# Sketch matrices loaded first, fewer zero matmuls, q in 256 B runs, single tasks for the q normalisation and new planner numbers, in a planned attention and channel-mix kernel

## The chip, the cores and the metric

The kernel runs on one core of one Trainium2 chip. The metric is device time in microseconds (us) of one execution. The span that a profile shows is about 1.8 us shorter than the time of the same execution (111.1 us of span against 112.87 us of time, for the kernel before). Engines are called PE (matmuls), PEld (PE's weight loads), DVE (vector), ACT (scalar), POOL (GpSimd) and SP (sync, which issues DMAs).

Executions of one kernel do not all take the same time here. The kernel before has runs of 112.4 to 113.8 us, fast, and others of 114.3 to 115.6 us, slow. The first measurements of before, from which the prediction started, were all of 114.2 us or more. The mean granted clock of a profile is given where it is below 0.99.

## The reference, cut to what matters

```python
# q, k, v: (4 batches, 4 heads, 1088 tokens, 32), float32; S1, S2: (8, 32)
def phi(x):                                   # 64 features a token
    a, b = x @ S1.T, x @ S2.T
    return outer(a, b).reshape(..., 64)
q_p, k_p = phi(q), phi(k)
kv, z = k_p.T @ v, sum(k_p, tokens)           # per batch and head
attn = (q_p @ kv) / (q_p @ z + 1e-6)
x = attn, heads side by side                  # (4, 1088, 128)
xk = mu_k * x + (1 - mu_k) * x_prev           # x_prev: the token before
xr = mu_r * x + (1 - mu_r) * x_prev
out = sigmoid(xr @ w_r) * (relu(xk @ w_k)**2 @ w_v)      # 128 -> 1024 -> 128
```

## The kernel before

All work is cut into tasks. A small planner in the Python program (a list scheduler) takes for each task an engine, a cost in us, the tasks it depends on and sometimes a due date, and fixes the order of instructions on every engine. In the traces an instruction that waits holds back what stands after it on its engine: in before, ACT waits 1.46 us for zm ahead of a small copy (kvs, 65.24 us), and PP behind that copy starts at 65.35, though its matmuls had ended at 64.9. The name of a task tells its stage: KT (transpose of k), KP (projection of k), KF (features), KA (accumulate kv), KZ and KW (fold), QT (transpose of q), Q1 (projection of q), QN (normalise), QF (features), QX (attention output), XK (mix with the token before), M1 and RE and SQ and M2 (the two large matmuls with relu and square between), FN (output). In profile lines the tiles have names of their own: kT and qT are the transposed k and q, ps_kab and ps_abw their projections, kp and qp their features, ps_kv the sums for kv, ps_qtp the transposed qp, ps_x the attention output, ps_r the product for the sigmoid, zm the masked sums for kv, pw the first product of the normalisation, PP and XB the two results of ACT from the attention output (XK, the mixed rows, is made from ps_x and PP), ps_h the result of the first large matmul, k its relu and square, ps_o that of the second large matmul, osb the output product, wt the target of the zero matmuls, sps and sp the first products of the sketch matrices S1 and S2.

```python
class Plan:
    LAT = {"PE": 0.16, "ACT": 0.20, "DVE": 0.14, "DMA": 0.0}
    ...
        for t in reversed(order):            # a due date is handed back to what it needs
            d = 1e9 if t["due"] is None else t["due"]
            for s in succ[t["name"]]:
                d = min(d, s["d"] - s["us"] - self.LAT[s["eng"]])
            t["d"] = d
    ...
                    r = max(r, t["d"] - window - t["us"])          # not before its window
                    key = (max(r, clock[e] + 0.02), t["d"], t["i"]) # then the earliest due

def load_q(b, eng):                          # 34 tokens of 32 floats in a row: 4352 B runs
    eng.dma_start(hdq[b][:], q[b].rearrange("h (a t) d -> (h a) t d", a=32))

load_k(0, nc.sync)
nc.scalar.dma_start(S8[:, 0, :], S1); nc.scalar.dma_start(S8[:, 1, :], S2)
load_v(0, nc.sync); load_q(0, nc.sync)
...
def q_trans(b, hf):                          # two a batch; output stride is 34 floats
    o = qT[:, b * S:(b + 1) * S].rearrange("p (a t) -> p t a", t=2 * U)
    nc.vector.transpose(o[:, U * hf:U * hf + U], hdq[b][:, U * hf:U * hf + U, :])

def q_norm(g):                               # one task: four dependent operations in a row
    nc.vector.tensor_mul(pw[:, :n, :, :R], x[:, :, :, 1], wsb[g][:, :n])
    nc.vector.tensor_reduce(den[:, :n], pw[:, :n], axis=AX, op=ADD)
    nc.vector.reciprocal(den[:, :n], den[:, :n])
    nc.vector.tensor_mul(an[:, :n], x[:, :, :, 1], _ap(d_, ...))

T0, PER = 14.0, 1.95
...     add(f"FN{g}", "DVE", dve(N), ..., due=T0 + PER * (G0[g] + n) + 4)
seq = plan.run(7.0)                          # the window
pe = 1.6
for t in seq:
    if t["eng"] == "PE":
        if t["start"] < WARM:                # zero matmuls fill PE's planned gaps
            for _ in range(max(0, int((t["start"] - pe - 0.1) / 0.23))):
                nc.tensor.matmul(wt[:], zero[:, :P], zero[:], skip_group_check=True)
        pe = t["start"] + t["us"]
    if t["fn"]:
        t["fn"]()
```

The zero matmuls write a PSUM bank that nobody reads. They are there to keep PE active, so that its matmuls run at their faster spacing when real work comes; in before's trace the zero matmuls themselves start 0.43 us apart at first and 0.22 after the ninth.

Of the kernel before, what the change touches and what calls it, by code (L numbers as in the profile page):

```python
# [27 lines left out]
class Plan:  # L28

    LAT = {"PE": 0.16, "ACT": 0.20, "DVE": 0.14, "DMA": 0.0}  # L30

# [15 lines left out]
    def run(self, window):  # L47
# [31 lines left out]
        n = 0  # L79
        while n < len(order):  # L80
            best = None
            for e, ts in todo.items():
                cand = None
                for t in ts:
                    r = max(clock[e], t.get("rel", 0.0))
                    for d in t["deps"]:
                        if d not in done:
                            r = None
                            break
                        r = max(r, done[d])  # L90
                    if r is None:
                        continue
                    if t["opens"]:
                        fb = free[t["opens"][0]]
                        if not fb:
                            continue
                        r = max(r, min(fb.values()))
                    r = max(r, t["d"] - window - t["us"])
                    key = (max(r, clock[e] + 0.02), t["d"], t["i"])
                    if cand is None or key < cand[0]:  # L100
                        cand = (key, t, r)
                if cand and (best is None or cand[2] < best[2]):
                    best = cand
# [36 lines left out]
def kernel(  # L140
# [39 lines left out]
    warm = const.tile([R, 1], F32)  # L180
    zero = const.tile([P, 512], BF16)
    nc.vector.memset(warm[:], 0.0)
    nc.vector.memset(zero[:], 0.0)
    nc.scalar.activation(warm[:], warm[:], SIGMOID)

    hdk = [const.tile([P, 2, U, D], F32, name=f"hdk{b}") for b in range(B)]
    hdq = [const.tile([P, 2 * U, D], F32, name=f"hdq{b}") for b in range(B)]
    vt = [const.tile([P, H, 9, D], F32, name=f"vt{b}") for b in range(B)]
# [5 lines left out]

    def load_q(b, eng):
        eng.dma_start(hdq[b][:], q[b].rearrange("h (a t) d -> (h a) t d", a=32))

    def load_v(b, eng):
        src = v[b].rearrange("h (p u) d -> p h u d", u=U)
        eng.dma_start(vt[b][:64], src[:, :, :9])  # L200
        eng.dma_start(vt[b][64:, :, :8], src[:, :, 9:])

    load_k(0, nc.sync)
    nc.scalar.dma_start(S8[:, 0, :], S1)
    nc.scalar.dma_start(S8[:, 1, :], S2)
    load_v(0, nc.sync)
    load_q(0, nc.sync)
    for b in range(1, B):
        load_k(b, nc.sync)
        load_v(b, nc.sync)  # L210
        load_q(b, nc.sync)

# [80 lines left out]
    SZ = H * S * D * 4 / BW  # L293
    t_ = 3.5
    arr = {}
    for b in range(B):
        for x in "kvq":
            t_ += SZ
            arr[x + str(b)] = t_
            if (b, x) == (0, "q"):  # L300
                t_ += 3.6
                arr["w"] = t_
# [7 lines left out]
    for x in range(2):  # L310
        nc.vector.tensor_copy(sel2[:, x, x], id8)
    hm = lambda ap: ap.rearrange("p (h d) -> p h d", h=H)
    sp = psum.tile([P, 512], F32, name="sps", tag="a0")
# [47 lines left out]
    def k_feat(b, gi, t0, t1):  # L361
        ab = kab[b, gi]
        if t0 == 0:
            kkp[b, gi] = work.tile([P, 5, H, R, R], F32, name="kp", tag="kp", bufs=3)
# [52 lines left out]
    for b in range(B):  # L417
        prev = []
        for gi, (t0, t1) in enumerate(KG):
            n = t1 - t0  # L420
            x = f"{b}_{gi}"
            add("KT" + x, "DVE", 0.13 + 0.00104 * (n * 128) + 0.1, lambda b=b, gi=gi: k_trans(b, gi), [f"Lk{b}"])
            add("KP" + x, "PE", 0.13 * n + 0.1, lambda b=b, gi=gi: k_proj(b, gi), ["KT" + x], opens=("aux", "kab_" + x))
            add("KE" + x, "ACT", act(64 * n), lambda b=b, gi=gi: k_evac(b, gi), uses=["kab_" + x])
            parts = [(0, 2), (2, n)] if n == 4 else [(0, 3), (3, n)]
            for j, (p0, p1) in enumerate(parts):
                add(f"KF{x}_{j}", "DVE", dve(256 * (p1 - p0)), lambda b=b, gi=gi, p0=p0, p1=p1: k_feat(b, gi, p0, p1), ["KE" + x])
                nm = f"KA{x}_{j}"
                add(nm, "PE", 0.17 * (p1 - p0) + 0.2, lambda b=b, gi=gi, p0=p0, p1=p1: k_acc(b, gi, p0, p1),
                    [f"KF{x}_{j}", f"Lv{b}"] + prev, **(dict(uses=[f"kv_{b}"]) if prev else dict(opens=("kv", f"kv_{b}"))))  # L430
# [8 lines left out]
    def q_trans(b, hf):  # L439
        o = qT[:, b * S:(b + 1) * S].rearrange("p (a t) -> p t a", t=2 * U)  # L440
        nc.vector.transpose(o[:, U * hf:U * hf + U], hdq[b][:, U * hf:U * hf + U, :])  # L441

    for b in range(B):
        for hf in range(2):
            add(f"QT{b}_{hf}", "DVE", 0.08 + 0.00104 * 32 * U, lambda b=b, hf=hf: q_trans(b, hf), [f"Lq{b}"])

# [14 lines left out]
    def q_evac(g):  # L461
        n = GS[g]
        wsb[g] = work.tile([P, 4, H, R], F32, name="wsb", tag="wsb", bufs=3)
        nc.scalar.copy(wsb[g][:, :n], abw(g)[:, :, :, 2])

    def q_norm(g):
        n = GS[g]
        x = abw(g)
        pw = pws[g % 2]
        nc.vector.tensor_mul(pw[:, :n, :, :R], x[:, :, :, 1], wsb[g][:, :n])  # L470
        den = work.tile([P, 4, H], F32, name="den", tag="den")
        nc.vector.tensor_reduce(den[:, :n], pw[:, :n], axis=AX, op=ADD)
        nc.vector.reciprocal(den[:, :n], den[:, :n])
        d_ = den[:, :n]
        an = work.tile([P, 4, H, R], F32, name="an", tag="an")
# [3 lines left out]
    def q_feat(g, t0, t1):  # L479
        if t0 == 0:  # L480
            qp[g] = work.tile([P, 4, H, R, R], F32, name="qp", tag="qp", bufs=3)
# [97 lines left out]

    T0, PER = 14.0, 1.95  # L580
    for g in range(NG):
# [3 lines left out]
        ns = len(bs)  # L585
        add(f"Q1{g}", "PE", 0.17 * n + 0.15, lambda g=g: q_proj(g), [f"QT{b}_{hf}" for b in bs for hf in range(2)] + [f"KW{b}" for b in bs],
            opens=("aux", f"abw_{g}"))
        add(f"QE{g}", "ACT", act(32 * n), lambda g=g: q_evac(g), uses=[f"abw_{g}"])
        add(f"QN{g}", "DVE", 2 * dve(32 * n) + dve(36 * n) + dve(32 * n) + 0.05, lambda g=g: q_norm(g), [f"QE{g}"], uses=[f"abw_{g}"])
        parts = [(0, 1), (1, 2)] if n == 2 else [(0, 2), (2, 4)]  # L590
        for j, (p0, p1) in enumerate(parts):
            add(f"QF{g}_{j}", "DVE", dve(256 * (p1 - p0)), lambda g=g, p0=p0, p1=p1: q_feat(g, p0, p1), [f"QN{g}"], uses=[f"abw_{g}"])
        for pair in range(2):
# [4 lines left out]
                [f"QR{g}_{pair}"], uses=[f"qtp_{g}_{pair}"])  # L598
        add(f"QX{g}", "PE", 0.215 * n + 0.15, lambda g=g: q_x(g), [f"QV{g}_0", f"QV{g}_1"] + [f"KB{b}" for b in bs], opens=("aux", f"x_{g}"))
        add(f"XP{g}", "ACT", act(N, True) + 0.05 * (ns - 1), lambda g=g: x_pp(g), ["Lw"], uses=[f"x_{g}"])  # L600
        add(f"XK{g}", "DVE", dve(N) + 0.06 * (ns - 1), lambda g=g: x_xk(g), [f"XP{g}"], uses=[f"x_{g}"])
        add(f"XB{g}", "ACT", act(N) + 0.05 * (ns - 1), lambda g=g: x_xb(g), uses=[f"x_{g}"])
        for c in range(8):
            add(f"M1{g}_{c}", "PE", N / 2400 + 0.01, lambda g=g, c=c: mm1(g, c), [f"XK{g}"], opens=("h", f"h_{g}_{c}"))
            add(f"RE{g}_{c}", "ACT", act(N), lambda g=g, c=c: relu(g, c), uses=[f"h_{g}_{c}"])
# [8 lines left out]
    for n_, x_ in plan_arr.items():  # L614
        plan.ids["L" + n_]["rel"] = x_
    seq = plan.run(7.0)


    wt = psum.tile([P, 512], F32, name="wt", tag="o0")
    WARM = 17.0  # L620
    pe = 1.6
    for t in seq:
        if t["eng"] == "PE":
            if t["start"] < WARM:
                for _ in range(max(0, int((t["start"] - pe - 0.1) / 0.23))):
                    nc.tensor.matmul(wt[:], zero[:, :P], zero[:], skip_group_check=True)  # L626
            pe = t["start"] + t["us"]
# [32 lines left out]
```

## Time and profile before

| | before |
|---|---|
| time, median (first three runs) | 114.81 us |
| profiled span | 111.1 us |
| first k projection starts on PE | 12.12 us |
| first q product starts on DVE (pw) | 20.23 us |
| after that to the end | 90.87 us, of which DVE is busy 74.69, PE 77.25, ACT 64.12 |

The page of the profile. Part 1 gives busy us, share of the span and instructions of each engine; part 2 gives for 40 equal slices the busy tenths (9 is 90% or more), PEclk being the granted clock of PE:

```profile
span 111.1 us, 3029 instructions
PE 91.5 (82%) x1243; PEld 59.8 (54%) x1243; DVE 84.7 (76%) x192; ACT 67.2 (61%) x166; POOL 9.1 (8%) x27
...
PE   0689976996999997899999975999768499898960
...
DVE  6280296699999999899999994678996347967860
ACT  5000200345869733899696357999536799898950
...
PEclk9999999999999999999999999999999999999999
DMA  3999999998001003000030030000302000300311
```

One slice is 2.8 us. DVE has idle slices at the start, is full from the 9th to the 24th slice, and has holes after that; in the last third no engine is full throughout. The loads keep the DMA engines busy for ten slices, to about 28 us.

The timeline of the first 21 us (start us, us from the first start to the last end, engine, line, operation, operands, count, and in brackets the idle time before and who ended it):

```profile
6.29 5.90 PE L626 MATMUL wt<-zero 128*128 128x512 bf16 x19
7.12 1.48 DVE L343 STREAM_TRANSPOSE kT<-hdk 128x256 f32<-128x256 f32 x4
...
12.12 1.27 PE L350 MATMUL ps_kab<-SW,kT 128*64 128x64 f32 x36
...
13.26 2.85 DVE L333 TENSOR_TENSOR kp<-ab 128x512 f32<-128x512 f32 x4 [4.65 <-ACT ab L357]
...
16.04 2.21 DVE L441 STREAM_TRANSPOSE qT<-hdq 128x544 f32<-128x544 f32 x2
18.09 0.18 DVE L392 TENSOR_TENSOR zm<-ps_kv,mask 128x32 f32<-128x32 f32 x1
...
20.23 0.23 DVE L470 TENSOR_TENSOR pw<-ps_abw,wsb 128x64 f32<-128x64 f32 x1 [0.90 <-ACT wsb L464]
```

PE is in 19 zero matmuls until 12.1 us while the transposed k lies ready from 8.6 us. DVE waits 4.65 us for that. Later zm stands behind both q transposes, though it needs only the kv matmuls.

The chain of waits, a stretch of the last third (start us, us, what):

```profile
63.91 1.06 DVE qp L333 x2
...
65.03 0.18 DVE zm L392
65.21 2.14 DVE qT L441 x2
67.34 0.65 DVE XK L517 x2
...
68.03 0.39 PE ps_h L530
```

And of the view of waits, PE's longest one after the start (who <- whom: us in total, times, longest):

```profile
PE ps_h L530 <- DVE XK L517: 4.3, 4, 2.0
```

Here two q transposes of the next batch (2.14 us) stand in DVE's order before XK, which the large matmuls wait for. XK starts when the second one ends, and PE stands idle for 2.0 us ahead of ps_h. XK also waits for ACT. The timeline of ACT and DVE there and at the next such wait, which has no transpose ahead of XK:

```profile
65.35 0.84 ACT L512 ACTIVATE PP<-ps_x,omu_k 128x384 f32<-128x384 f32 x2
67.18 0.81 DVE L517 SCALAR_TENSOR_TENSOR XK<-ps_x,mu_k,PP 128x384 bf16<-128x384 f32 x2
...
85.27 0.84 ACT L512 ACTIVATE PP<-ps_x,omu_k 128x448 f32<-128x448 f32 x2 [0.44 <-PE ps_x L506]
86.68 0.88 DVE L517 SCALAR_TENSOR_TENSOR XK<-ps_x,mu_k,PP 128x448 bf16<-128x448 f32 x2 [1.50 <-ACT XB L523]
```

With DVE idle and ready, XK started 1.41 us after the start of its PP; behind the two transposes, 1.83 us after. So an estimate of the transposes' share in the 2.0 us is 0.4 us; the wait at 87.6 us, without them, was 1.6 us long.

Groups (busy us, mean ns of one | idle before them):

```profile
L542 DVE TENSOR_TENSOR k<-k 128x1024 bf16<-128x1024 bf16 (+1 forms) x40 | 23.6, 604 | 7.3 <-ACT k L536 6.6
L441 DVE STREAM_TRANSPOSE qT<-hdq 128x544 f32<-128x544 f32 x8 | 9.0, 1189 | 0.0
```

### The profile page before, as it was taken

What the parts mean: (1) busy time and instruction counts of PE and PEld (TensorE: products, weight loads), DVE (VectorE), ACT (ScalarE), POOL (GpSimd) and SP (SyncE); (2) the same over time, 40 slices, a digit from 0 to 9 for tenths busy, and PEclk for the clock granted to TensorE, in tenths of its full rate; (3) what the DMA queues carried; (4) which work ended last, traced back from release to release, by engine and by line L of the source; (5) the groups of instructions that cost most, each with busy time, mean ns of one, the idle gap of its engine ahead of it and who ended that gap; (6) DMA issues with size and microseconds to landing.
All of it is one profiled execution on the core that took longest, in us unless ns stands there. A gap on an engine that the chain in (4) does not pass through costs nothing.

```text
span 111.1 us, 3029 instructions
## 1 busy us (share of the span) xinstructions
PE 91.5 (82%) x1243; PEld 59.8 (54%) x1243; DVE 84.7 (76%) x192; ACT 67.2 (61%) x166; POOL 9.1 (8%) x27
## 2 busy tenths in 40 slices
PE   0689976996999997899999975999768499898960
PEld 0434562555466784638777753467645247366530
DVE  6280296699999999899999994678996347967860
ACT  5000200345869733899696357999536799898950
POOL 7390290000000000000000000000000000000000
PEclk9999999999999999999999999999999999999999
DMA  3999999998001003000030030000302000300311
GB/s 100 268 293 290 252 344 254 332 269 205 26 6 47 0 6 94 0 9 0 0 100 0 6 94 0 0 0 6 94 5 89 0 0 6 97 0 1 93 56 47
DMA packets 9166, 9.70 MB, mean 87 GB/s; under 512 B 1584, under 2 KB 7984, under 8 KB 9152
## 3 DMA queue, kind: packets, MB, share of 16 engines
q1 hardware_dynamic: 7840, 8.91, 28.1%
q0 software_dynamic: 1280, 0.59, 3.8%
q8 instruction: 10, 0.16, 0.7%
q14 instruction: 4, 0.03, 0.1%
q10 hardware_dynamic: 32, 0.00, 0.0%
HBM read 7.80 MB, written 2.23 MB: 90 GB/s over the span
## 4 chain that ended last, share of the span: by engine, by line
DVE 43%; PE 28%; ACT 18%; issue 5%; DMA 2%; DVEq 0%; ACTq 0%
ACT k L536 11%; DVE k L542 7%; DVE kp L333 7%; DVE qT L441 6%; PE wt L626 6%; DVE qp L333 5%; PE ps_h L530 4%; PE ps_x L506 4%; PE ps_o L552 3%; DVE osb L577 3%; DVE XK L517 3%; ACT PP L512 3%; DVE kT L343 3%; PE ps_kab L350 3%; DMA S<-in_S_dram 2%
## 5 line engine op out<-in xcount | busy, mean ns | idle before, releaser
L536 ACT ACTIVATE k<-ps_h 128x512 bf16<-128x512 f32 (+1 forms) x80 | 36.7, 558 | 3.4 <-PE ps_h L530 3.2
L542 DVE TENSOR_TENSOR k<-k 128x1024 bf16<-128x1024 bf16 (+1 forms) x40 | 23.6, 604 | 7.3 <-ACT k L536 6.6
L530 PE MATMUL ps_h<-XK,wk 128*128 128x512 bf16 (+1 forms) x80 | 21.9, 348 | 4.6 <-DVE XK L517 4.3
L552 PE MATMUL ps_o<-wv,k 128*128 128x128 bf16 x272 | 21.6, 220 | 1.6 <-DVE k L542 1.4
L552 PEld LDWEIGHTS <-k 128*128 128x128 bf16 x272 | 16.4, 98 | 7.6 <-DVE k L542 4.7
L333 DVE TENSOR_TENSOR kp<-ab 128x512 f32<-128x512 f32 (+1 forms) x16 | 11.7, 756 | 4.7 <-ACT ab L357 4.7
L530 PEld LDWEIGHTS <-wk 128*128 128x128 bf16 x80 | 6.6, 98 | 11.4 <-issue 9.4
L357 ACT COPY ab<-ps_kab 128x256 f32<-128x256 f32 (+1 forms) x8 | 3.3, 406 | 15.7 <-PE ps_kab L350 15.7
L489 PE MATMUL ps_qtp<-ident,qp 128*128 128x128 f32 x68 | 10.9, 283 | 1.9 <-DVE qp L333 1.2
L498 ACT COPY qpT<-ps_qtp 128x512 f32<-128x512 f32 (+1 forms) x18 | 9.2, 549 | 5.1 <-PE ps_qtp L489 5.1
L333 DVE TENSOR_TENSOR qp<-an,ps_abw 128x512 f32<-128x512 f32 (+1 forms) x20 | 11.2, 599 | 0.1
L489 PEld LDWEIGHTS ps_qtp<-ident,qp 128*128 128x128 f32 x68 | 7.3, 140 | 4.4 <-DVE qp L333 1.3
L517 DVE SCALAR_TENSOR_TENSOR XK<-ps_x,mu_k,PP 128x512 bf16<-128x512 f32 (+7 forms) x13 | 6.9, 552 | 3.5 <-ACT XB L523 2.2
L506 PE MATMUL ps_x<-qpT,kvbd 128*64 128x512 f32 (+7 forms) x52 | 9.5, 462 | 0.0
L378 PE MATMUL ps_kv<-kp,vt 128*32 128x64 f32 x288 | 7.2, 224 | 2.5 <-DVE kp L333 2.3
L441 DVE STREAM_TRANSPOSE qT<-hdq 128x544 f32<-128x544 f32 x8 | 9.0, 1189 | 0.0
L626 PE MATMUL wt<-zero 128*128 128x512 bf16 x28 | 8.5, 450 | 0.0
L512 ACT ACTIVATE PP<-ps_x,omu_k 128x512 f32<-128x512 f32 (+7 forms) x13 | 6.8, 548 | 2.5 <-PE ps_x L506 2.5
L454 PE MATMUL ps_abw<-SW,qT 128*64 128x96 f32 x136 | 7.6, 253 | 0.0
L378 PEld LDWEIGHTS ps_kv<-kp,vt 128*32 128x32 f32 x288 | 4.8, 109 | 5.1 <-DVE kp L333 4.1
L454 PEld LDWEIGHTS ps_abw<-SW,qT 128*64 128x64 f32 x136 | 5.9, 136 | 2.0 <-issue 0.6
L577 DVE TENSOR_TENSOR osb<-ps_o,r 128x512 f32<-128x512 f32 (+1 forms) x10 | 6.0, 604 | 0.8 <-PE ps_o L552 0.8
(69 smaller groups left out, 100.7 us busy)
## 6 DMA issues: line engine op xcount, KB each, us to landing
hdk<-in_k_dram SPq DMA_DIRECT2D x4, 544.0 KB, 9.7
hdq<-in_q_dram SPq DMA_DIRECT2D x4, 544.0 KB, 10.8
out_dram<-osb SPq DMA_DIRECT2D x7, 256.0 KB, 2.3
vt<-in_v_dram SPq DMA_DIRECT2D x4, 288.0 KB, 9.7
vt<-in_v_dram SPq DMA_DIRECT2D x4, 256.0 KB, 12.3
out_dram<-osb SPq DMA_DIRECT2D x3, 128.0 KB, 2.5
wk<-in_moe_w_k_dram POOLq DMA_DIRECT2D x1, 256.0 KB, 7.2
wv<-in_moe_w_v_dram POOLq DMA_DIRECT2D x1, 256.0 KB, 15.4
```

Of the source, the lines that this page charges most:

```text
L333: nc.vector.tensor_mul(o.rearrange("p t h i j -> p (t h) i j"), _ap(a_, [[sa, y], [1, R], [0, R]]), _ap(b_, [[sb, y], [0, R], [1, R]]))
L378: nc.tensor.matmul(kv[32 * h:32 * h + 32, :64], vt[b][:, h, T, :], kp[:, t, h].rearrange("p i j -> p (i j)"), start=(T == 0), stop=(T == 8 ...
L441: nc.vector.transpose(o[:, U * hf:U * hf + U], hdq[b][:, U * hf:U * hf + U, :])
L454: nc.tensor.matmul(p[64 * c:64 * c + 64, t * 96:t * 96 + 96], qT[:, s:s + 64], SW[:, s // S].rearrange("p h x r -> p (h x r)"), skip_group ...
L489: nc.tensor.transpose(p[:, t * P:t * P + P], qp[g][:, t, 2 * pair:2 * pair + 2].rearrange("p h i j -> p (h i j)"), ident[:])
L506: nc.tensor.matmul(p[64 * pair:64 * pair + 64, c0:c0 + m], kvbd[:, b, pair, :], qpT[g][:, pair, c0:c0 + m], skip_group_check=True, tile_po ...
L517: nc.vector.scalar_tensor_tensor(XK[:, s:s + m], tiles[f"x_{g}"][:, c0:c0 + m], mu_k[:], PP[:, c:c + m], op0=MUL, op1=ADD)
L530: nc.tensor.matmul(h[:, :n * P], wk[:, c * P:(c + 1) * P], XK[:, G0[g] * P:(G0[g] + n) * P])
L536: nc.scalar.activation(k1s[g, c // 2][:, c % 2, :n * P], tiles[f"h_{g}_{c}"][:, :n * P], RELU)
L542: nc.vector.tensor_mul(k2[:, :, :n * P], k1[:, :, :n * P], k1[:, :, :n * P])
L552: nc.tensor.matmul(o[:, t * P:t * P + P], k2s[g, j][:, c, t * P:t * P + P], wv[:, 2 * j + c, :], start=(j == 0 and c == 0 and t == 0), sto ...
L626: nc.tensor.matmul(wt[:], zero[:, :P], zero[:], skip_group_check=True)
```

## The change

Its intent: begin the serial start earlier, make the q transposes cheaper and smaller, let other work in between the small operations of the normalisation, and give the planner numbers meant to be nearer to the chip's.

```diff
-    LAT = {"PE": 0.16, "ACT": 0.20, "DVE": 0.14, "DMA": 0.0}
+    LAT = {"PE": 0.24, "ACT": 0.18, "DVE": 0.15, "POOL": 0.15, "DMA": 0.0}
+    OWN = {"PE": 0.0, "ACT": 0.15, "DVE": 0.12, "POOL": 0.12, "DMA": 0.0}
...
-                        r = max(r, done[d])
+                        r = max(r, done[d] - (self.LAT[e] - self.OWN[e] if self.ids[d]["eng"] == e else 0.0))
...
-        eng.dma_start(hdq[b][:], q[b].rearrange("h (a t) d -> (h a) t d", a=32))
+        for h in range(H):
+            engs[h % len(engs)].dma_start(hdq[b][32 * h:32 * h + 32].rearrange("a t c d -> a t (c d)"),
+                                          q[b, h].rearrange("(t a c) d -> a t (c d)", a=32, c=2))
...
+    nc.sync.dma_start(S8[:, 0, :], S1)
+    nc.scalar.dma_start(S8[:, 1, :], S2)
     load_k(0, nc.sync)
-    nc.scalar.dma_start(S8[:, 0, :], S1)
-    nc.scalar.dma_start(S8[:, 1, :], S2)
...
+    dummy(4)                     # four zero matmuls ahead of the sketch products
...
-        o = qT[:, b * S:(b + 1) * S].rearrange("p (a t) -> p t a", t=2 * U)
-        nc.vector.transpose(o[:, U * hf:U * hf + U], hdq[b][:, U * hf:U * hf + U, :])
+        o = qT[:, b * S:(b + 1) * S].rearrange("p (t a c) -> p t c a", a=32, c=2)
+        t0, t1 = QSP[hf]
+        nc.vector.transpose(o[:, t0:t1], hdq[b][:, t0:t1])
+    QSP = [(0, 4), (4, 9), (9, 13), (13, 17)]
...
-        add(f"QN{g}", "DVE", ..., lambda g=g: q_norm(g), ...)
+        add(f"QP{g}", ...); add(f"QD{g}", ...); add(f"QI{g}", ...); add(f"QN{g}", ...)
...
-    T0, PER = 14.0, 1.95
+    T0, PER = 8.0, 1.5
...                              # several task costs, for instance KP 0.13n -> 0.102n
-    seq = plan.run(7.0)
+    seq = plan.run(5.0)
...
-    WARM = 17.0
-    pe = 1.6
+    WARM = 14.0
+    pe = 4.4                     # 5 zero matmuls ahead of the first projection, where 19 were
```

A q projection now also waits only for the transposes whose tokens it needs.

More of the change, by code (lines that the diff above doesn't have):

```diff
@@ L181 @@
     zero = const.tile([P, 512], BF16)
+    nc.vector.memset(zero[:], 0.0)
     nc.vector.memset(warm[:], 0.0)
-    nc.vector.memset(zero[:], 0.0)
     nc.scalar.activation(warm[:], warm[:], SIGMOID)
     hdk = [const.tile([P, 2, U, D], F32, name=f"hdk{b}") for b in range(B)]
-    hdq = [const.tile([P, 2 * U, D], F32, name=f"hdq{b}") for b in range(B)]
+    hdq = [const.tile([P, U, 2, D], F32, name=f"hdq{b}") for b in range(B)]
     vt = [const.tile([P, H, 9, D], F32, name=f"vt{b}") for b in range(B)]
@@ L193, in load_k, with load_q @@
         eng.dma_start(hdk[b][:], k[b].rearrange("h (a c u) d -> (h a) c u d", a=32, c=2))
-    def load_q(b, eng):
-        eng.dma_start(hdq[b][:], q[b].rearrange("h (a t) d -> (h a) t d", a=32))
+    def load_q(b, engs):
+        for h in range(H):
+            engs[h % len(engs)].dma_start(hdq[b][32 * h:32 * h + 32].rearrange("a t c d -> a t (c d)"),
+                                          q[b, h].rearrange("(t a c) d -> a t (c d)", a=32, c=2))
     def load_v(b, eng):
@@ L201, in load_v @@
         eng.dma_start(vt[b][64:, :, :8], src[:, :, 9:])
+    nc.sync.dma_start(S8[:, 0, :], S1)
+    nc.scalar.dma_start(S8[:, 1, :], S2)
     load_k(0, nc.sync)
-    nc.scalar.dma_start(S8[:, 0, :], S1)
-    nc.scalar.dma_start(S8[:, 1, :], S2)
     load_v(0, nc.sync)
-    load_q(0, nc.sync)
+    load_q(0, [nc.sync, nc.scalar])
     for b in range(1, B):
@@ L210 @@
         load_v(b, nc.sync)
-        load_q(b, nc.sync)
+        load_q(b, [nc.sync])
     ident = const.tile([P, P], F32)
@@ L293 @@
     SZ = H * S * D * 4 / BW
-    t_ = 3.5
+    t_ = 3.2
     arr = {}
@@ L297 @@
         for x in "kvq":
-            t_ += SZ
+            t_ += SZ * (1.3 if x == "q" else 1)
             arr[x + str(b)] = t_
@@ L311, with dummy @@
         nc.vector.tensor_copy(sel2[:, x, x], id8)
+    wt = psum.tile([P, 512], F32, name="wt", tag="o0")
+    def dummy(n):
+        for _ in range(n):
+            nc.tensor.matmul(wt[:], zero[:, :P], zero[:], skip_group_check=True)
+    dummy(4)
     hm = lambda ap: ap.rearrange("p (h d) -> p h d", h=H)
@@ L362, in k_feat @@
         ab = kab[b, gi]
-        if t0 == 0:
+        if (b, gi) not in kkp:
             kkp[b, gi] = work.tile([P, 5, H, R, R], F32, name="kp", tag="kp", bufs=3)
@@ L421 @@
             x = f"{b}_{gi}"
-            add("KT" + x, "DVE", 0.13 + 0.00104 * (n * 128) + 0.1, lambda b=b, gi=gi: k_trans(b, gi), [f"Lk{b}"])
-            add("KP" + x, "PE", 0.13 * n + 0.1, lambda b=b, gi=gi: k_proj(b, gi), ["KT" + x], opens=("aux", "kab_" + x))
+            add("KT" + x, "DVE", 0.19 + 0.00104 * (n * 128), lambda b=b, gi=gi: k_trans(b, gi), [f"Lk{b}"])
+            add("KP" + x, "PE", 0.102 * n + 0.1, lambda b=b, gi=gi: k_proj(b, gi), ["KT" + x], opens=("aux", "kab_" + x))
             add("KE" + x, "ACT", act(64 * n), lambda b=b, gi=gi: k_evac(b, gi), uses=["kab_" + x])
@@ L428 @@
                 nm = f"KA{x}_{j}"
-                add(nm, "PE", 0.17 * (p1 - p0) + 0.2, lambda b=b, gi=gi, p0=p0, p1=p1: k_acc(b, gi, p0, p1),
+                add(nm, "PE", 0.1 * (p1 - p0) + 0.1, lambda b=b, gi=gi, p0=p0, p1=p1: k_acc(b, gi, p0, p1),
                     [f"KF{x}_{j}", f"Lv{b}"] + prev, **(dict(uses=[f"kv_{b}"]) if prev else dict(opens=("kv", f"kv_{b}"))))
@@ L439, in q_trans @@
     def q_trans(b, hf):
-        o = qT[:, b * S:(b + 1) * S].rearrange("p (a t) -> p t a", t=2 * U)
-        nc.vector.transpose(o[:, U * hf:U * hf + U], hdq[b][:, U * hf:U * hf + U, :])
+        o = qT[:, b * S:(b + 1) * S].rearrange("p (t a c) -> p t c a", a=32, c=2)
+        t0, t1 = QSP[hf]
+        nc.vector.transpose(o[:, t0:t1], hdq[b][:, t0:t1])
+    QSP = [(0, 4), (4, 9), (9, 13), (13, 17)]
     for b in range(B):
-        for hf in range(2):
-            add(f"QT{b}_{hf}", "DVE", 0.08 + 0.00104 * 32 * U, lambda b=b, hf=hf: q_trans(b, hf), [f"Lq{b}"])
+        for hf in range(4):
+            add(f"QT{b}_{hf}", "DVE", 0.09 + 0.00104 * 64 * (QSP[hf][1] - QSP[hf][0]), lambda b=b, hf=hf: q_trans(b, hf), [f"Lq{b}"])
     qp, qpT, wsb = {}, {}, {}
@@ L464, in q_evac, with q_pw, q_den, q_rec @@
         nc.scalar.copy(wsb[g][:, :n], abw(g)[:, :, :, 2])
+    dens = {}
+    def q_pw(g):
+        n = GS[g]
+        nc.vector.tensor_mul(pws[g % 2][:, :n, :, :R], abw(g)[:, :, :, 1], wsb[g][:, :n])
+    def q_den(g):
+        n = GS[g]
+        dens[g] = work.tile([P, 4, H], F32, name="den", tag="den")
+        nc.vector.tensor_reduce(dens[g][:, :n], pws[g % 2][:, :n], axis=AX, op=ADD)
+    def q_rec(g):
+        d_ = dens[g][:, :GS[g]]
+        nc.vector.reciprocal(d_, d_)
     def q_norm(g):
@@ L468, in q_norm @@
         x = abw(g)
-        pw = pws[g % 2]
-        nc.vector.tensor_mul(pw[:, :n, :, :R], x[:, :, :, 1], wsb[g][:, :n])
-        den = work.tile([P, 4, H], F32, name="den", tag="den")
-        nc.vector.tensor_reduce(den[:, :n], pw[:, :n], axis=AX, op=ADD)
-        nc.vector.reciprocal(den[:, :n], den[:, :n])
-        d_ = den[:, :n]
+        d_ = dens[g][:, :n]
         an = work.tile([P, 4, H, R], F32, name="an", tag="an")
@@ L479, in q_feat @@
     def q_feat(g, t0, t1):
-        if t0 == 0:
+        if g not in qp:
             qp[g] = work.tile([P, 4, H, R, R], F32, name="qp", tag="qp", bufs=3)
@@ L578, in fin, with qts @@
         nc.sync.dma_start(orow[G0[g] * P:(G0[g] + n) * P].rearrange("(t p) f -> p t f", p=P), o[:, :n])
-    T0, PER = 14.0, 1.95
+    def qts(g):
+        res = []
+        for b, _, s, m in segs(g):
+            lo, hi = (s - b * S) // 64, (s - b * S + m) // 64
+            res += [f"QT{b}_{i}" for i, (t0, t1) in enumerate(QSP) if t0 < hi and t1 > lo]
+        return res
+    T0, PER = 8.0, 1.5
     for g in range(NG):
@@ L585 @@
         ns = len(bs)
-        add(f"Q1{g}", "PE", 0.17 * n + 0.15, lambda g=g: q_proj(g), [f"QT{b}_{hf}" for b in bs for hf in range(2)] + [f"KW{b}" for b in bs],
+        add(f"Q1{g}", "PE", 0.165 * n + 0.12, lambda g=g: q_proj(g), qts(g) + [f"KW{b}" for b in bs],
             opens=("aux", f"abw_{g}"))
         add(f"QE{g}", "ACT", act(32 * n), lambda g=g: q_evac(g), uses=[f"abw_{g}"])
-        add(f"QN{g}", "DVE", 2 * dve(32 * n) + dve(36 * n) + dve(32 * n) + 0.05, lambda g=g: q_norm(g), [f"QE{g}"], uses=[f"abw_{g}"])
+        add(f"QP{g}", "DVE", dve(32 * n), lambda g=g: q_pw(g), [f"QE{g}"], uses=[f"abw_{g}"])
+        add(f"QD{g}", "DVE", dve(36 * n), lambda g=g: q_den(g), [f"QP{g}"])
+        add(f"QI{g}", "DVE", 0.07 + 0.0083 * 4 * n, lambda g=g: q_rec(g), [f"QD{g}"])
+        add(f"QN{g}", "DVE", dve(32 * n), lambda g=g: q_norm(g), [f"QI{g}"], uses=[f"abw_{g}"])
         parts = [(0, 1), (1, 2)] if n == 2 else [(0, 2), (2, 4)]
@@ L598 @@
                 [f"QR{g}_{pair}"], uses=[f"qtp_{g}_{pair}"])
-        add(f"QX{g}", "PE", 0.215 * n + 0.15, lambda g=g: q_x(g), [f"QV{g}_0", f"QV{g}_1"] + [f"KB{b}" for b in bs], opens=("aux", f"x_{g}"))
+        add(f"QX{g}", "PE", 0.213 * n + 0.12, lambda g=g: q_x(g), [f"QV{g}_0", f"QV{g}_1"] + [f"KB{b}" for b in bs], opens=("aux", f"x_{g}"))
         add(f"XP{g}", "ACT", act(N, True) + 0.05 * (ns - 1), lambda g=g: x_pp(g), ["Lw"], uses=[f"x_{g}"])
@@ L603 @@
         for c in range(8):
-            add(f"M1{g}_{c}", "PE", N / 2400 + 0.01, lambda g=g, c=c: mm1(g, c), [f"XK{g}"], opens=("h", f"h_{g}_{c}"))
+            add(f"M1{g}_{c}", "PE", N / 2400 + 0.003, lambda g=g, c=c: mm1(g, c), [f"XK{g}"], opens=("h", f"h_{g}_{c}"))
             add(f"RE{g}_{c}", "ACT", act(N), lambda g=g, c=c: relu(g, c), uses=[f"h_{g}_{c}"])
@@ L615 @@
         plan.ids["L" + n_]["rel"] = x_
-    seq = plan.run(7.0)
-    wt = psum.tile([P, 512], F32, name="wt", tag="o0")
-    WARM = 17.0
-    pe = 1.6
+    seq = plan.run(5.0)
+    WARM = 14.0
+    pe = 4.4
     for t in seq:
@@ L624 @@
             if t["start"] < WARM:
-                for _ in range(max(0, int((t["start"] - pe - 0.1) / 0.23))):
-                    nc.tensor.matmul(wt[:], zero[:, :P], zero[:], skip_group_check=True)
+                dummy(max(0, int((t["start"] - pe - 0.15) / 0.25)))
             pe = t["start"] + t["us"]
```

## The prediction

> **What bounds the kernel now.** The profiled span is 111.1 us (timed median 114.81). The page shows PE 82% busy (8.5 us of it zero matmuls), DVE 76%, ACT 61%. By stage (timeline and windows):
>
> 1. 0 to 21 us, a serial start. DVE ends the first k transposes by 8.6 us, but PE is in 19 zero matmuls from 6.3 to 12.1 us (about 430 ns apart at first), so the first k projection starts at 12.12 us and DVE idles 4.65 us until 13.26 us (waits: kp after ab). Then both q transposes (2.21 us) stand in DVE's order before zm, which starts at 18.09 us although the last kv matmuls start at 16.4. The first q product on DVE starts at 20.23 us.
> 2. 20 to 68 us: DVE is saturated (9.4 to 9.9 of every 10 us up to 60).
> 3. 68 to 111 us: nobody is saturated throughout; the chain alternates ACT relu, DVE squares, PE. DVE idles up to 1.6 us at a time, waiting for ACT.
>
> **What the change does.**
> - Fewer zero matmuls stand before the first k projection: 4 before the sketch products, 5 after. The projection then starts about 8.0 us, not 12.1: 4 us off the critical path.
> - Sketch matrices first: sps starts at 3.75 us, DVE's selector ends at 3.44, so at most 0.3 us, perhaps 0.5 more if the sketch products run warm. The skill (TensorE: Matmul & The Clock Gate, "What's actually happening") says that activity releases the throttle, after a window of about 3.4 us; the trace agrees roughly: spacing falls from 430 to about 215 ns some 3.5 us into the zeros.
> - q transposes: 8 of 1189 ns (stride 34 elements) become 16 with stride 2, like kT's (391 to 404 ns for 256 elements; 0.47 for 320, an estimate). 1.7 instead of 2.4 us a batch: 2.8 us less DVE work, 2.1 in the saturated stretch. zm now stands after only two of four, worth about 1.2 us more in the start.
> - Single normalisation tasks: dependent small operations leave gaps of 0.03 to 0.05 us and lose their overlap (a 128x512 product takes 0.60 us pipelined, 0.68 in its record). Interleaving gives perhaps 0.5 us.
> - Cost: q arrives in 2176 packets of 256 B a batch instead of 256 of 4352 B. The trace's 512 B packets take 27 ns; at an estimated 20 ns, q takes 2.7 instead of 1.7 us a batch: 4 us more DMA, ending near 32 instead of 28 us, off the critical path because k2, k3 and q1 to q3 wait in SBUF. The first q, on two queues, should land near 10 us, before its use near 12.
> - Other planner latencies and window reorder everything: unknown, about +-3 us.
>
> **Critical path.** Start about 5 us (first pw near 15 us), saturated stretch 2, gaps 0.5; the tail, where PE and ACT count as much, gives a little back.
>
> **Prediction: 107.8 us, range 103.5 to 112.0.** Faster by over 2%: 0.87; within 2%: 0.10; slower: 0.03.
>
> **What would show it.** First ps_kab near 8 us; first kp near 9.2; first pw near 15; q transposes near 0.40 us each, 6.7 in sum; DVE busy about 82 us; DMA full until about 32; DVE idle before the first kp under 1.5 us; from the fourth zm to the end still about 46 us.
>
> **What would make it wrong.** 256 B packets much slower than 20 ns, so that k, v or w_v land late (w_v is closest: 22.5 us, needed about 25); the reordered tail idling more, or overlapping much better (under 104); PE at half clock at the start.

## The result, and the profile after

The result is correct and takes 103.91 us (median of 4 runs, 102.99 to 104.58, the last of them marked slow), against 114.69 us for the kernel before in the same group. Ratios are the mean time of one kernel's fast runs over that of the other's of the same rounds, so not quite the ratio of the medians: here 0.9033, 95% interval 0.8956 to 0.911. In that group all four runs of before took 114.2 us or more. A second group, in which before also had its runs near 112.8 us, gave 0.9183 (0.905 to 0.9316) for the same two kernels, and is the fairer of the two. The profiled spans are 111.1 and 101.2 us, both at a mean clock of 1.0: 9.9 us less.

The page after, the same lines as before:

```profile
span 101.2 us, 3018 instructions
PE 88.0 (87%) x1222; PEld 58.5 (58%) x1229; DVE 80.0 (79%) x200; ACT 67.6 (67%) x166; POOL 7.2 (7%) x27
...
PE   5988893989999997899989999999887999896750
...
DVE  5374959999899978999999985889983667794450
ACT  5002031468769746996499699989658999895830
...
DMA  1999999999999953000210030003011000221101
```

The holes of the last third are shallower on PE, and the loads now last into the 15th slice of 2.5 us, to 36.8 us by the packet records. The start:

```profile
5.65 2.32 PE L319 MATMUL wt<-zero 128*128 128x512 bf16 x5
...
7.90 1.87 PE L360 MATMUL ps_kab<-SW,kT 128*64 128x64 f32 x36
...
9.47 2.76 DVE L343 TENSOR_TENSOR kp<-ab 128x512 f32<-128x512 f32 x4 [1.51 <-ACT ab L367]
...
12.16 0.83 DVE L452 STREAM_TRANSPOSE qT<-hdq 128x256 f32<-128x256 f32 x2
...
12.91 0.15 DVE L402 TENSOR_TENSOR zm<-ps_kv,mask 128x32 f32<-128x32 f32 x1
...
15.03 0.22 DVE L482 TENSOR_TENSOR pw<-ps_abw,wsb 128x64 f32<-128x64 f32 x1 [0.90 <-ACT wsb L476]
```

The projection starts at 7.90 instead of 12.12 us, zm follows two short q transposes instead of two long ones, and pw starts 5.2 us earlier. The chain of waits where the fourth zm and the XK of the same group as above now stand is on PE, which has ps_qtp and ps_r matmuls to run while XK is made; in the view of waits, PE's loss to XK has fallen:

```profile
58.71 0.59 PE ps_qtp L511 x4
...
59.76 0.22 PE ps_h L552
59.97 0.05 issue
60.03 0.38 PE ps_h L552
60.41 0.36 PE ps_kv L388 x16
60.77 0.06 PE ps_kv L394 x4
60.83 1.01 PE ps_x L528 x4
```

```profile
PE ps_h L552 <- DVE XK L539: 0.9, 2, 0.7
```

```profile
L564 DVE TENSOR_TENSOR k<-k 128x1024 bf16<-128x1024 bf16 (+1 forms) x40 | 23.6, 603 | 6.2 <-ACT k L558 5.8
L452 DVE STREAM_TRANSPOSE qT<-hdq 128x256 f32<-128x256 f32 (+1 forms) x16 | 6.7, 436 | 0.0
```

From pw to the end it is 86.17 us where it was 90.87 (the windows view), so 4.7 us of the 9.9 come after the start. In these stretches DVE's busy time fell by 3.9 us, and its idle time by 0.8; PE's busy time fell by 1.8 and its idle time by 2.9. Which of these is cause and which only follows, the profile does not tell: both engines are over 80% busy. The experiments have to.

### The profile page after: what moved, and what is told of

It is laid out like the page before. It is cut to its first block, busy times and chain, and to the rows that moved or that the text cites. A ratio compares the mean times of both kernels' runs of the same rounds, so it can differ in the third digit from the quotient of the medians.

```text
span 101.2 us, 3018 instructions
## 1 busy us (share of the span) xinstructions
PE 88.0 (87%) x1222; PEld 58.5 (58%) x1229; DVE 80.0 (79%) x200; ACT 67.6 (67%) x166; POOL 7.2 (7%) x27
## 4 chain that ended last, share of the span: by engine, by line
PE 58%; DVE 19%; ACT 16%; issue 4%; ACTq 0%; DVEq 0%
PE ps_o L574 11%; PE ps_h L552 10%; ACT k L558 9%; PE ps_x L528 6%; PE ps_qtp L511 5%; PE ps_kab L360 5%; PE wt L319 5%; PE ps_abw L466 5%; DVE k L564 4%; PE ps_kv L388 3%; DVE kp L343 3%; DVE XK L539 3%; ACT PP L534 3%; ACT XB L545 2%; DVE qT L452 2%
## 5 line engine op out<-in xcount | busy, mean ns | idle before, releaser
L558 ACT ACTIVATE k<-ps_h 128x512 bf16<-128x512 f32 (+1 forms) x80 | 37.3, 563 | 2.1 <-PE ps_h L552 1.8
L574 PE MATMUL ps_o<-wv,k 128*128 128x128 bf16 x272 | 20.9, 220 | 1.4 <-DVE k L564 1.4
L520 ACT COPY qpT<-ps_qtp 128x512 f32<-128x512 f32 (+1 forms) x18 | 9.8, 579 | 2.8 <-PE ps_qtp L511 2.7
L360 PE MATMUL ps_kab<-SW,kT 128*64 128x64 f32 x144 | 6.6, 242 | 1.7 <-DVE kT L353 1.7
L360 PEld LDWEIGHTS ps_kab<-SW,kT 128*64 128x64 f32 x144 | 5.6, 153 | 3.6 <-issue 2.7
L592 ACT ACTIVATE r<-ps_r 128x512 f32<-128x512 f32 (+1 forms) x10 | 5.6, 556 | 1.7 <-PE ps_r L587 1.7
```

The source lines that it names most:

```text
L360: nc.tensor.matmul(p[64 * c:64 * c + 64, (t - t0) * 64:(t - t0) * 64 + 64], kT[b][:, t, 64 * c:64 * c + 64], SW[:, 0, :, :2, :], skip_grou ...
L520: nc.scalar.copy(o, i)
L558: nc.scalar.activation(k1s[g, c // 2][:, c % 2, :n * P], tiles[f"h_{g}_{c}"][:, :n * P], RELU)
L574: nc.tensor.matmul(o[:, t * P:t * P + P], k2s[g, j][:, c, t * P:t * P + P], wv[:, 2 * j + c, :], start=(j == 0 and c == 0 and t == 0), sto ...
```

## The experiments

The twelve runs use the kernels above: a control without any edit, ten runs with one change each and a last one with two. In those that touch the order, the zero matmuls are held at fixed counts for each task (after's: 4 at first, 5 before the first KP, then 1, 1, 2, 1), so that another plan does not change them as well. "Order held" means that the order of instructions on each engine is the same as in the kernel it starts from.

The runs came in four groups on three chips. The control was in one of them only (with the three other rows on q's load and layout); it was expected near a ratio of 0.905 and had 0.9183, because before also had fast runs there. Marked slow, and so not in the ratios, are one of four runs of "no first zeros", two of four of "old q layout" and two of four of "one task to normalise". Two runs of one kernel at a clock of 1.0 differed by up to 0.8 us in span (105.8 and 105.0 with 19 zeros), so single spans are not exact to tenths. Against the control's interval, only 19 zeros, the old planner numbers, the old due dates and the due dates of 1.1 us stand clear of noise; for the others the size rests on single profiles.

| run | what | ratio to before (95%) | profiled span |
|---|---|---|---|
| after again (control) | | 0.9183 (0.905 to 0.932) | 101.2 |
| before, 5 zeros | order held | 0.9792 (0.968 to 0.991) | 107.8 |
| after, 19 zeros | order held | 0.9526 (0.943 to 0.963) | 105.8 |
| after, no first zeros | order held | 0.9172 (0.907 to 0.927) | 101.5 |
| after, old planner numbers | planned again | 0.9492 (0.943 to 0.955) | 105.1 |
| after, old due dates only | planned again | 0.9609 (0.955 to 0.967) | 107.7 |
| after, old q layout | planned again | 0.9307 (0.907 to 0.954) | 102.5 |
| after, q in 4352 B runs | order held | 0.9208 (0.913 to 0.929) | 101.7 |
| after, stride 34 | order held | 0.9246 (0.917 to 0.933) | 102.1 |
| after, one task to normalise | planned again | 0.9250 (0.915 to 0.935) | 102.0 |
| after, due dates 1.1 us | planned again | 0.8848 (0.878 to 0.892) | 98.2 |
| the same, 3 zeros | order held | none | 96.7 |

### The start: zero matmuls

In the kernel before:

```diff
-  for _ in range(max(0, int((t["start"] - pe - 0.1) / 0.23))):   # 19 ahead of KP0_0
+  for _ in range({'KP0_0': 5, 'KA0_0_0': 1, 'KD0': 3, 'Q10': 1, 'KP1_0': 4}.get(t["name"], 0)):
```

> The kernel before, with one edit: 5 zero matmuls instead of 19 ahead of the first k projection (order of all other instructions as before). Theory A (the start is serial and its gain is carried to the end): the first ps_kab starts near 8.2 us instead of 12.1 and the run takes 110.7 us, about 4.0 us less than before. Rival B (the later stages absorb an earlier start, because PE, ACT and DVE wait for each other there, and the gain of the change lies in its order): less than 2 us gained, above 112.7 us.

Measured: 110.35 us (median), ratio 0.9792. In the profile the whole schedule moved: pw starts at 16.91 instead of 20.23 us, the first output product at 30.41 instead of 33.76, and the last at 104.35 instead of 107.67. The shift is 3.3 us in all three places. The timeline of this run shows why it is not 4.0, as expected; the projection starts at 8.45 instead of the expected 8.2 us, and then:

```profile
6.20 2.32 PE L626 MATMUL wt<-zero 128*128 128x512 bf16 x5
...
8.44 2.00 PEld L350 LDWEIGHTS ps_kab<-SW,kT 128*64 128x64 f32 x36 [0.84 <-issue]
8.45 2.19 PE L350 MATMUL ps_kab<-SW,kT 128*64 128x64 f32 x36
```

The projection takes 2.19 us where it took 1.27, because PE is still at its slow spacing (0.1 us from pair to pair of matmuls, where it was 0.06).

The other way round, in the kernel after:

```diff
-  dummy(max(0, int((t["start"] - pe - 0.15) / 0.25)))     # 5 ahead of KP0_0
+  dummy({'KP0_0': 19, 'KA0_0_0': 1, 'KA0_1_0': 1, 'KD0': 2, 'Q10': 1}.get(t["name"], 0))
```

> The kernel after, with 19 zero matmuls instead of 5 ahead of the first k projection. Theory A: PE is held until about 11.7 us instead of 7.9, and the run takes 107.6 us, 3.7 more than after's 103.9. Rival B: less than 1.5 us lost, under 105.5.

Measured: 107.37 us, and span 105.8 where after has 101.2. The first projection starts at 12.38 us, the first output product at 32.55 instead of 27.81, the last at 102.58 instead of 98.03: 4.6 us later to the end. The first kp and pw are 4.05 us later; by the ratios of the fast runs the loss is 3.9 us, so the 0.5 us on top is of this one profile. Both runs speak for theory A and against an absorbing tail, the first by its profile only (by its interval the gain is anything from 1.1 to 3.6 us), the second by its times too: in a fixed order a shift of the start arrived at the end nearly whole.

### The four zero matmuls at the very beginning

```diff
-    dummy(4)
```

> The kernel after without the 4 zero matmuls ahead of the sketch products. My theory (they fill time in which PE waits for the sketch matrices anyway, and only bring PE's faster matmuls forward): the first ps_kab still starts near 7.9 us, but its 36 matmuls and the first kv matmuls run at the slow spacing for longer, 2.2 us instead of 1.9 for ps_kab; 0.3 to 0.8 us slower than after. Rival: no difference beyond 0.2 us in the first kp, pw and the span.

Measured: 103.8 us (profile at a clock of 0.970), ratio 0.9172, the same as the control's 0.9183. The timeline of the run without them:

```profile
7.89 2.19 PE L359 MATMUL ps_kab<-SW,kT 128*64 128x64 f32 x36
...
9.47 2.77 DVE L342 TENSOR_TENSOR kp<-ab 128x512 f32<-128x512 f32 x4 [1.50 <-ACT ab L366]
```

The projection took 2.19 instead of 1.87 us, as expected, but kp starts at the same 9.47 us, and pw at 15.02. The first half of the projection, which kp waits for, ran at the slow spacing in both. So my expected 0.3 to 0.8 us was wrong and the rival right: this part of the change is worth nothing that can be measured here.

### The planner's numbers

```diff
-    LAT = {"PE": 0.24, ...}; OWN = {...}          # and the line that uses OWN
+    LAT = {"PE": 0.16, "ACT": 0.20, "DVE": 0.14, "DMA": 0.0}
-    T0, PER = 8.0, 1.5 ... plan.run(5.0)
+    T0, PER = 14.0, 1.95 ... plan.run(7.0)        # and the task costs of before
```

> The kernel after, with the planner's numbers of before (latencies, task costs, window 7.0, due dates), the zero matmuls held at after's counts; q's layout, quarter transposes and single tasks stay. Theory A (the planner's numbers remove the idle time after 60 us that my prediction missed): about 107 us, 3 more than after, with PE idle again ahead of the first ps_h of a group. Rival C (short q transposes and less DVE work remove it, the numbers matter little): within 1 us of 103.9.

Measured: 106.8 us, ratio 0.9492, span 105.1. pw starts at 15.35 us, near after's 15.03, and the fourth output product is even earlier (56.19 against 57.78). The fifth is later (69.60 against 66.95), and the last is 3.9 us later. As much waiting for XK as in the kernel before is back, in the view of waits of this run:

```profile
PE ps_h L551 <- DVE XK L538: 4.3, 4, 1.5
```

This is theory A as far as the size goes, and rival C falls: short transposes alone do not remove the holes. But it is the same sum of waits in other places, not the same wait. Ahead of the four XK here stand a small copy (SW) or osb, no q transposes; before the XK at 80.00 us DVE itself sits idle for 2.1 us until ACT has made XB. And the sum is no measure of the loss: in the run with one task to normalise PE waits 2.5 us for XK, and its span is only 0.8 us longer than after's. Which of the numbers?

```diff
-    T0, PER = 8.0, 1.5
+    T0, PER = 14.0, 1.95
```

> The kernel after with one line of the planner undone: the due dates of the output groups (first 14.0 us and 1.95 us a token tile, as before, instead of 8.0 and 1.5). Latencies, task costs and window stay those of after. Theory F (of the planner's numbers it is the due dates that matter: late due dates rank the front work of the next batch ahead of what the groups of now wait for): about 3.5 us slower than after, near 107, like the run with all old numbers. Rival G (the latencies, costs and window matter): within 1 us of after, 103 to 105.

Measured: 108.47 us, ratio 0.9609. The profiled run had a mean clock of 0.976 and a span of 107.7; the three others, at 0.996 to 1.0, had 106.4 to 106.9. So the late due dates with the other new numbers are worse, by about 5 us, than after, and worse than all old numbers together. That is outside what either theory said (3.5 us, or within 1), so the numbers do not simply add: with the old due dates, the new latencies, costs and window made the kernel slower. The due dates alone are worth as much as that here; the other numbers were not undone alone, so what they are worth beside the new due dates is not shown. PE waits for XK 2.7 us and for the q features (qp) 2.6 us in this run.

The same line, further in the other direction:

```diff
-    T0, PER = 8.0, 1.5
+    T0, PER = 8.0, 1.1
```

> The kernel after with its due dates pulled further in the same direction (8.0 us and 1.1 us a tile instead of 1.5), nothing else. Theory F: 2 to 5 us faster than after, about 100; the bubbles on PE and DVE in the last 40 us shrink further. Rival G: within 1 us of after, or slower, because after's numbers were already the best of this kind.

Measured: 99.76 us, ratio 0.8848, span 98.2, against 101.2 of after. From pw to the end it is 83.2 us with DVE busy 70.5 of them; after had 86.2 with 70.8. So nothing became cheaper; 2.7 us of DVE idle time went. The line of the squares in the groups after has 6.2 us of idle before it; here it is:

```profile
L564 DVE TENSOR_TENSOR k<-k 128x1024 bf16<-128x1024 bf16 (+1 forms) x40 | 23.9, 600 | 2.9 <-ACT k L558 2.7
```

The direction was as theory F expected, but its reason, that late due dates put the front work of the next batch first, is the wrong way round. With 1.95, 1.5 and 1.1 us the first output product started at 26.4, 27.8 and 32.5 us, and the fourth zm at 64.5, 60.9 and 58.1 us: earlier due dates bring the work of later batches forward and let the first outputs wait. The replay of the planner shows by what: a task may not start before its due date less the window, and with 1.95 us this holds back nine entries of the plan, among them all loads of k, v and q of the third and fourth batch, and so whatever needs these loads (the loads themselves are issued at the start in any case); with 1.5 us it holds back two, with 1.1 us none. That this early work then fills the holes at the end fits the profile, but no run tests it alone. The planner's own end time, which could be read before any run, had the same order: 99.4, 94.2 and 88.6 us.

This order asks for k of the third batch sooner, and meets the loads, as DVE's timeline shows:

```profile
25.91 0.77 DVE L353 STREAM_TRANSPOSE kT<-hdk 128x256 f32<-128x256 f32 x2 [1.14 <-DMA hdk<-in_k_dram]
```

### q in 256 B runs, the stride, and the pieces

Undoing all of q's part, planned again with the costs that go with it (the cuts of code below are shortened):

```diff
-  dma_start(hdq[b][32*h:32*h+32] "a t c d -> a t (c d)", q[b, h] "(t a c) d -> a t (c d)")
+  dma_start(hdq[b][32*h:32*h+32] "a t c d -> a (t c d)", q[b, h] "(a t) d -> a (t d)")
-    QSP = [(0, 4), (4, 9), (9, 13), (13, 17)]             # output stride 2
+    QSP = [(0, 9), (9, 17)]                                # output stride 34; Q1 waits for both
```

> The kernel after with q's part of the change undone: 4352 B runs, output stride of 34 elements, two transposes a batch, first q products waiting for both of them; planned again with that cost, zero matmuls held. Theory A (the cheaper and smaller q transposes are worth about their 2.8 us of DVE time): 2 to 3 us slower than the control, about 106.4. Rival B (PE, not DVE, sets the pace of after, so q's layout is worth little): within 0.7 us of the control.

Measured: 105.7 us (two runs of four marked slow; the fast ones are 104.31 and 105.52), ratio 0.9307 against 0.9183 with wide intervals; span 102.5 against 101.2. So it is worth about 1.3 us, below the 2 to 3 of theory A and above the 0.7 of rival B. PE's wait for XK is 2.8 us in this run, 0.9 in after.

The DMA cost alone. The load has long runs; the values land in wrong places, so the result is wrong:

```diff
-  dma_start(hdq[b][32*h:32*h+32] "a t c d -> a t (c d)", q[b, h] "(t a c) d -> a t (c d)")
+  dma_start(hdq[b][32*h:32*h+32] "a t c d -> a (t c d)", q[b, h] "(a t) d -> a (t d)")
```

> The kernel after, every instruction in the same order, but q is loaded in runs of 4352 B into the same tile: the values land in the wrong places, so the result is wrong on purpose. It takes away the cost of the 256 B runs alone. Theory A (the loads are ahead of their use): the loads end near 28 us instead of 37, and the time stays within 0.5 us of the control. Rival E (late k, v or w_v hold after back): over 1 us faster than the control.

Measured: 103.78 us, ratio 0.9208 against the control's 0.9183. The loads ended at 32.3 us instead of 36.8 (not near 28, as expected; the many smaller DMAs are still there), so the 256 B runs cost 4.5 us of loading, and taking them away helped nothing. The profiled span, at a clock of 0.974, is even 0.5 us longer, most of it from one stop of 0.4 us on PE at 26.8 us whose cause the profile does not name ("issue"). Rival E falls for this order: the loads are ahead of their use.

The stride alone (wrong; q's tile is zeroed first, since the quarters now write places that others read before they are complete):

```diff
-        o = qT[...].rearrange("p (t a c) -> p t c a", a=32, c=2);  transpose(o[:, t0:t1], ...)
+        o = qT[...].rearrange("p (a t) -> p t a", t=2 * U);        transpose(o[:, 2*t0:2*t1], ...)
```

> The kernel after, every instruction in the same order, but the q transposes write with a stride of 34 elements again (16 of them; q's tile is zeroed first on GpSimd; the result is wrong on purpose). It adds the stride's cost alone. Theory A: each transposes about 0.53 us instead of 0.35 of DVE's order, 2.8 us in sum, and 1.5 to 2.8 us slower than the control. Rival B (PE sets the pace): under 0.8 us slower.

Measured: 104.12 us, ratio 0.9246; span 102.1, 0.9 us more than after. The transposes did cost what was expected, by the group's line of this run (after had 6.7 us, 436 ns):

```profile
L454 DVE STREAM_TRANSPOSE qT<-hdq 128x256 f32<-128x256 f32 (+1 forms) x16 | 10.0, 667 | 0.0
```

DVE's busy time rose from 80.0 to 82.4 us, but the span by only 0.9. Theory A expected 1.5 to 2.8, rival B under 0.8; the truth lies just above B. Half of it, 0.46 us, is there at the first pw (15.49 us), so in the rest of the kernel 1.7 us of added DVE time (70.8 to 72.5) cost 0.4 us. DVE time was not fully on the critical path in after's order; before's was not tested for this.

### One task for the normalisation

```diff
-  add("QP"...); add("QD"...); add("QI"...); add("QN"...)
+  add("QN", "DVE", ..., lambda: (q_pw(g), q_den(g), q_rec(g), q_norm(g)))
```

> The kernel after, with the four operations of the q normalisation in one task again (so they stand next to each other on DVE). Theory A: gaps of 0.03 to 0.05 us and lost overlap come back, ten groups of four: 0.5 to 1 us, so 104.4 to 104.9. Rival D (single tasks let other work in between at the places where PE waits): over 2 us lost, above 106.

Measured: 105.32 us as a median, but two of its four runs are marked slow; the two fast ones are 103.78 and 104.67, the ratio 0.925, and the span 102.0 against 101.2. The size is that of theory A (0.5 to 1 us) and excludes rival D's 2 us; the interval overlaps the control's, so 0.8 us is shown by one profile only.

### A version that beats both

The due dates of 1.1 us a tile, with 3 zero matmuls instead of 5 ahead of the first projection:

> The version meant to beat both kernels: after's due dates at 1.1 us a tile, and 3 zero matmuls instead of 5 ahead of the first k projection, so that PE is free near 7.05 us when the first k transposes end (7.2 us), where after starts the projection at 7.9. Theory A (a fixed order passes a shift of the start on to the end): first kp near 8.75 us instead of 9.46, span 97.5 instead of the 98.2 of the run with 1.1 us and 5 zeros, time near 99.1. Rival: PE at the slow spacing for longer eats the 0.7 us, span 98.0 or more.

Measured: correct, 98.59 us (median of 6, 98.06 to 99.45); before took 115.26 as a median in these rounds, 112.48 at its fastest. The span is 96.7 us, 1.5 less than with 5 zeros. The first kp starts at 8.86 us (expected 8.75), the first pw at 14.57 instead of 15.01, so only 0.4 us of the start is left by then. The reason is on PE's timeline of this run:

```profile
9.94 0.43 PE L388 MATMUL ps_kv<-kp,vt 128*32 128x64 f32 x16 [0.32 <-DMA vt<-in_v_dram]
```

The first kv matmuls now wait for v. The rest of the 1.5 us shows first where the third k arrives: DVE starts to transpose it at 24.38 instead of 25.91 us. That this k arrived sooner than in the other run was not caused by the zero matmuls as far as I can show, so I claim 0.4 us for them and leave the rest open: the medians differ by 1.2 us on two chips, and the runs of either version spread over 1.3 us or more. Both versions are faster than before in their groups, and below the runs of after in the others; after was not run beside them.

## Why the prediction was right or wrong

The direction was right, and the time is inside the range, at its lower edge: 107.8 predicted, 103.5 to 112.0 the range, 103.91 measured. The gain was 7.0 us as predicted from 114.81, 10.8 measured in that group's medians, 9.9 in the spans of two profiles at full clock. Part of the 3.9 us between prediction and result is the base: 7.0 us were taken from 114.81, a time in the range that later groups mark slow, while the profile that was read belongs to a run of 112.87 us. From that the same sum gives 105.9, and in the fairer group before and after differ by about 9.3 us (ratio 0.9183). So the sum was too small by about 2.3 us, and which state the first runs were in was not foreseen; that the time still fell inside the range says little of the parts.

- **The start ("about 5 us", "first ps_kab near 8", "first kp near 9.2", "first pw near 15")** was right: 7.90, 9.47 and 15.03 us, and pw 5.2 us earlier. The split was a little off. Fewer zeros were called 4 us; alone in before they gave 3.3, because PE runs the projection at the slow spacing and starts it at 8.45 us. The sketch matrices were called "at most 0.3 us"; sps starts at 3.08 instead of 3.75 us. The step that failed there: I took the end of DVE's second selector (3.44 us) as the limit, but sps needs only the first one, ready at 3.05. Against before with 5 zeros, kp starts 0.55 us earlier (9.47 and 10.02), and from kp to zm it is 3.44 us instead of 4.74: the 1.3 us of zm's new place, called 1.2. These two are read from timelines, not tried apart.
- **"Perhaps 0.5 more if the sketch products run warm"** did not happen: their records are as long as before (0.79 and 1.11 us), and the zeros ahead of them were worth nothing.
- **q transposes ("2.8 us less DVE work, 2.1 in the saturated stretch"; "saturated stretch 2")** were right in cost (6.7 us in sum predicted and measured, 436 ns each by the records) and wrong in worth. With the order held, 2.4 us more of DVE time cost 0.9 us of span. The step that failed: I took an engine that is busy 96% for the only one that sets the pace, while PE is 93% busy in the same stretch (38.6 and 37.1 of 40 us from 20 to 60 us). The fourth output product came 5.45 us earlier, only 0.25 us more than the first pw, so up to there the 2 us did not appear, as far as two different orders can be compared. After the change PE carries 58% of the chain of waits, where it had 28%.
- **Single tasks ("perhaps 0.5 us")**: 0.8 us by one profile.
- **DMA ("at an estimated 20 ns", "DMA full until about 32")**: the cost of the packets was nearly right, 4.5 us by the run with long ones where 4 was called (27 ns in the median for q's 256 B packets on SP's queue, 18 ns on ACT's). The loads lasted to 36.8 us because of two things that the sum left out: before's own end is 29.9, not 28, and the loads in more and smaller DMAs with long runs still ended at 32.3. (The "256 of 4352 B" are 128 a batch.) It was off the critical path, as predicted, in after's order; in the order with early due dates it is not.
- **"Other planner latencies and window reorder everything: unknown, about +-3 us"** and **"the tail ... gives a little back"**: this is the term that was mis-sized. The planner's numbers are worth 3.9 us of span, all after 60 us, in the favourable direction. "From the fourth zm to the end still about 46 us" came out as 40.3 (60.88 to 101.2). This mark also moved: the q transposes of the last batch, behind the fourth zm in before (65.13 us), start at 46.75 us in after. From the mark to the end DVE is busy 27.3 instead of 31.2 us and idle 13.0 instead of 14.9. I called this term unknown and the tail a small loss; the order of the new kernel could be read and the planner replayed before predicting, and neither was done. Which decision of the planner is worth what stays open, beyond the due dates.

The single effects (3.3, about 1.9 for the rest of the start, 0.9, 0.8, 3.9) sum to more than 9.9 us, and q's part undone as a whole is 1.3: effects of order overlap, so they are not shares of the gain. The normalisation's 0.8 us in this sum rests on one profile.

## What to carry to other kernels

In a planned order, ask for each long task that is not urgent what stands directly behind it on its engine, and check when that one would have been ready: zm behind two long transposes lost about 1.3 us by the timelines, XK behind two others only about 0.4 of the 2.0 us that the chain of waits suggests. Replay the planner before predicting, and see what its window holds back. The due date of an output is a strong lever of a list scheduler, and one line to try: here 1.95 (with a first date of 14 us instead of 8), 1.5 and 1.1 us a tile gave 108.5, 103.9 and 99.8 us with all else as in the new kernel. A start-up shift passed to the end almost whole where the order was fixed; filler work that only exists to speed up an engine should end about when the first real work is ready.

## What the Trainium skill lacked or had wrong

- TensorE: Matmul & The Clock Gate, section "What's actually happening", gives a window of about 3.4 us of activity before the faster spacing, and says that the window is free-running. The runs fit this, with a spread: counted from the first of the zeros that run without a gap, the faster spacing begins 3.4 us later in before (6.29 to 9.7 us), 3.6 us later in after (5.65 to 9.25, inside the projection, whose first 16 matmuls take 1.08 us in the chain of waits, where before they took 0.64) and 5.2 us later in the run with 19 zeros (5.66 to 10.9). What of the earlier work counts as activity (PE is also occupied from 1.18 to 4.92 us in after), the page does not tell, and no run here settles it.
- Trace reading: the profile's row PEclk reads 9 in all slices of both kernels, including those in which zeros are 0.43 us apart. The slow spacing has to be read from the timeline; the page on TensorE only warns that the clock events of traces have been seen to be unreliable.
- SBUF — State Buffer, section "Door 1: The DMA port swizzle", says that accesses that stay in one 16-byte line run at full rate and those that cross to a new one pay, "4 fp32" being free. The runs fit this for DVE's 32x32 transposes and add a size: with an output stride of 2 floats a record is 436 ns in the mean, with 34 floats 667 ns; strides between were not run. VectorE: DVE Perf Modes, section "The three transpose paths", gives one time for the transpose and none by stride.
- DMA: Bandwidth & Descriptors, section "Specifications", sets the least transfer for full rate at 512 B. No such step comes out of these packet records. In after, 256 B packets took 27 ns in the median on SP's queue and 18 ns on ACT's (9.5 and 14 B a ns), the 512 B stores 27 ns (19) and v's loads in 1024 B packets 81 ns (13). What the 256 B runs cost as a whole is shown: loads to 36.8 us, with long runs in the same order to 32.3.
